# A decode attention backward kernel: scores by wide matmuls in four column groups, and another split of ten stores over the DMA engines

## The chip, the core and the metric

The kernel runs on one core of one Trainium2 chip. The metric is the device time of one execution in microseconds; the medians given are over ten runs. A core has a tensor engine (PE, with its weight loads shown apart as PEld), a vector engine (DVE), a scalar engine (ACT), GpSimd (POOL) and a sync engine (SP), and 16 DMA engines that move data between the HBM and the on-chip buffer. In this kernel SP issues the loads and POOL issues the stores. Matmul results land in a separate memory, PSUM[...].

## What is computed

The reference is the gradient of single-query attention. With 2 x 32 = 64 heads, one query row per head, 8192 keys and 128 elements per row, all in bfloat16, it returns the attention output and the gradients of q, k and v:

```python
def _fwd_reference(q, k, v):
    scale = q.shape[-1] ** -0.5
    scores = jnp.einsum("bhqd,bhkd->bhqk", q, k) * scale
    p = _softmax(scores, axis=-1)
    return jnp.einsum("bhqk,bhkd->bhqd", p, v)

def reference(q, k, v, grad_out):
    ...
    _out, _vjp = jax.vjp(_f, q, k, v)
    _grads = _vjp(grad_out)
```

Written out for one head: s = K q, E = exp(scale (s - max s)), l = sum E, p = E / l, dp = V g with g the row of grad_out, delta = sum(p dp), dS = p (dp - delta). The outputs are o = p V, dq = scale dS K, dk = scale dS q (an outer product, 8192 x 128) and dv = p g (likewise). K and V are read once, dk and dv written once: 268 MB each way.

## The kernel before

A head's K or V is one tile `kvt` of 128 partitions x 64 rows x 128 elements, 2 MB; partition p holds the keys 64 p to 64 p + 63. There are 12 such buffers (`NTILE`). A tile is loaded by one DMA of SP (`load`, L98), read by PE for the scores and for dq or o, then overwritten in place by DVE with the outer product dk or dv (`outer`, L394), and stored from there by one DMA of POOL (L412). The load of a later head waits for the store of the buffer that it takes. All instructions stand in program order on their engines (`pin`), and each engine runs its own queue in that order.

Time goes in slots: eight per head (`SL`), four for the K tile and four for the V tile, each on a chunk of 16 of the 64 row blocks. In a slot g the loop at L423 emits, in this order: loads that come due, one outer product of an earlier head, 16 PE transposes of the chunk into PSUM and one ACT copy to `ev` (`transpose_chunk`, L184 and L186), the partial sums for dq or o of an earlier head (`acc`, L339), the exponent (`expo`) when due, and the scores of the chunk of the slot before (`score_chunk`, L195). After these come the steps that are due once a head: maximum (`max_part`, `max_all`, `max_spread`), sums and weights (`normalise_p`, `weigh`, `normalise_ds`), and picking the dq or o sums out of PSUM (`pick`, then `join` two slots later).

The scores: each of the 16 transposed blocks in `ev` is loaded as weights and multiplied by the one column of q (or g) in `qdT`, 16 weight loads and 16 matmuls of one column a slot. The result for a chunk is 16 columns in the bank `sw` (scores) or `dpw` (dp), already in the layout in which the exponent wants them.

The sums for dq and o (`acc`): per slot four matmuls with 512 columns, whose weights are 64 columns of E or dS, taken from a zero-padded copy (`E_pad`, `dS_pad`); they go by turns to two groups of 64 output columns (`CW`, `NG`). `pick` takes the diagonal blocks out of the 512 columns with the 0/1 columns of `diag`, and `join` sums them over partitions.

Stores: eight of the 64 dk stores (`SPREAD`: heads 4, 11, ... 53) are issued in two parts by `by_rows` (L87), 126 partition rows and 2; all others are whole. The very first DMA of POOL resets the cursor from which its DMAs choose engines, and loads 6 rows of q (`FIRST`, L108 to L110). The last head's two tiles are stored in four pieces each by SP. At the end dq and o are transposed and each stored by one DMA of SP from 64 partitions (L489).

Of the kernel before, what the change touches and what calls it, by code (L numbers as in the profile page):

```python
# [13 lines left out]

CH = 16
QT = 4
CW = 64
NG = 2
NTILE = 12
FIRST = 6  # L20
SPREAD = range(4, 60, 7)

@with_exitstack
def kernel(
# [110 lines left out]
    nc.vector.memset(E_pad[:], 0.0)  # L136
    nc.vector.memset(dS_pad[:], 0.0)

    qdT = const.tile([P, 2, BH], BF16)
    for w in range(2):  # L140
        tps = ps_m.tile([P, BH], BF16, tag=f"acc{w}", name="tps")
        nc.tensor.transpose(tps[:], qd_nat[:BH, w, :], ident_bf[:BH, :BH])
        nc.vector.tensor_copy(out=qdT[:, w, :], in_=tps[:])

    dqT = const.tile([P, BH], BF16)
    oT = const.tile([P, BH], BF16)

    def begin_s(i):

        h = heads[i]  # L150
        sw = ps_sdp.tile([P, NT + P + 1], F32, tag="s", name="sw")
        h.s = sw[:, 0:NT]
        h.mT = sw[0:1, NT : NT + P]
        h.mb = sw[:, NT + P :]

    def begin_dp(i):

        h = heads[i]
        dpw = ps_sdp.tile([P, NT + 2 + D], F32, tag="dp", name="dpw")
        h.dp = dpw[:, 0:NT]  # L160
        h.lsum = dpw[:, NT : NT + 2]
        h.qbp = dpw[:, NT + 2 :]

    def broadcast(i, w):

        h = heads[i]
        pin(
            nc.tensor.matmul(  # L168
                h.qbp,
                lhsT=qdT[:, w, i : i + 1].to_broadcast([P, P]),  # L170
                rhs=ident_bf[:],
                start=True,
                stop=True,
            )
        )
        h.qb[w] = small.tile([P, D], BF16, tag=f"qb{w}", name="qb")
        pin(nc.vector.tensor_copy(out=h.qb[w][:], in_=h.qbp))  # L177
# [9 lines left out]
        return ev  # L187

    def score_chunk(i, c, ev):
        h = heads[i]  # L190
        w, c = divmod(c, NCH)
        dst = h.dp if w else h.s
        for t in range(CH):
            pin(
                nc.tensor.matmul(  # L195
                    dst[:, c * CH + t : c * CH + t + 1],
                    lhsT=ev[:, t, :],
                    rhs=qdT[:, w, i : i + 1],
                    start=True,
                    stop=True,  # L200
                )
            )
# [185 lines left out]
    def outer(i, w, c, ends):  # L388

        h = heads[i]  # L390
        n0 = c * CH
        shape = [P, CH, D // 2, 2]
        pin(
            nc.vector.tensor_tensor(  # L394
                out=h.tile[w][:, n0 : n0 + CH, :].rearrange("p n (e t) -> p n e t", t=2),
                in0=h.qb[w][:]
                .rearrange("p (e t) -> p e t", t=2)
                .unsqueeze(1)
                .to_broadcast(shape),
                in1=h.pair[w][:, n0 : n0 + CH, :].unsqueeze(2).to_broadcast(shape),  # L400
                op=ALU.mult,
            )
        )
        if c + 1 in ends:
            at = ends.index(c + 1)
            b0, b1 = (ends[at - 1] if at else 0) * CH, (c + 1) * CH
            dst = (dv_v if w else dk_v)[i]
            if w == 0 and i in SPREAD:
                by_rows(store_eng, dst, h.tile[w], (P - 2, 2))
            else:  # L410
                eng = load_eng if len(ends) > 1 else store_eng
                pin(eng.dma_start(out=dst[:, b0:b1, :], in_=h.tile[w][:, b0:b1, :]))  # L412
# [10 lines left out]
    for g in range(SL * BH + O0 + NCH + 4 - SL):  # L423
# [3 lines left out]
        def at(r0):  # L427

            return next((i for i, r in now if r == r0), None)
# [49 lines left out]
        if (i := at(A1 + NCH)) is not None:  # L479
            pick(i, 1)  # L480
# [39 lines left out]
```

## Time and profile before

| | us |
|---|---|
| median of 10 runs | 1286.93 |
| lowest, highest | 1285.25, 1289.36 |
| the profiled execution | 1284.91 |
| its span, first to last instruction | 1283.1 |

The profiled execution's time is 1.8 us over its span. The span is what views of the trace are timed in. The mean granted TensorE clock was 0.956.

| group | busy us | count, mean ns |
|---|---|---|
| L186 ACT copies of the transposed chunks | 954.4 | 512, 1865 |
| L394 DVE outer products | 621.9 | 512, 1215 |
| L184 PE transposes | 561.0 | 8192, 223 |
| L339 PE sums for dq and o | 168.6 + 159.9 | 2 x 1024, 412 and 393 |
| L195 PE scores | 141.9 + 140.7 | 2 x 4096, 164 |
| L362 DVE picking | 134.7 | 384, 351 |

The mean length of a PE record is longer than its share of busy time, because matmuls overlap in the pipeline. Queues of DMAs are named q0 (issued by POOL), q1 (issued by SP) and q8 (instructions); each is served by all 16 DMA engines at once, in packets of at most 16 KB, so that a whole load or store is 128 packets, eight for each engine. The page gives the mean busy share of the 16 engines in tenths for 40 slices of the span. A busy share by slice is a mean over the engines: it does not say whether one of them has more to do than another.

### The profile page before, as it was taken

The numbers are of one execution on the slowest core, as the hardware profiler recorded it, in microseconds if no ns is written. First come the engines' busy times: TensorE is split into PE (matmuls) and PEld (weight loads), VectorE is DVE, ScalarE is ACT, GpSimd is POOL, SyncE is SP. The second block draws the span as 40 slices with busy tenths as digits, with TensorE's granted clock in tenths as the row PEclk, the third lists the DMA queues.
The fourth block names the chain that finished last, engine by engine and source line by source line (L and its number), as shares of the span: only waits on it lengthen the run. The fifth ranks groups of instructions, "written<-read, shape, count | busy, mean of one in ns | idle before, by whom it ended". The sixth has DMA issues, their size and how long they took to land.

```text
span 1283.1 us, 42576 instructions
## 1 busy us (share of the span) xinstructions
PE 1131.4 (88%) x19268; PEld 860.5 (67%) x19268; DVE 936.0 (73%) x2122; ACT 975.2 (76%) x641; POOL 76.0 (6%) x143
## 2 busy tenths in 40 slices
PE   6999999999998989898888898897889899989881
PEld 5777777667766766676666676675667667767660
DVE  2888888778777867686777677776768677777773
ACT  6888888778777877786777787786778677777760
POOL 0000000000000000000000000000000000000000
PEclk9999999999999989998999999998999899999895
DMA  9999999999999999999999999999999999999996
GB/s 388 424 427 426 428 428 427 427 428 424 429 428 424 418 426 428 428 421 427 426 430 424 425 428 428 426 423 428 426 427 426 425 428 428 423 425 427 428 404 265
DMA packets 40194, 539.68 MB, mean 421 GB/s; under 512 B 5196, under 2 KB 5196, under 8 KB 6476
## 3 DMA queue, kind: packets, MB, share of 16 engines
q1 hardware_dynamic: 20172, 272.70, 49.9%
q0 software_dynamic: 19840, 264.25, 48.8%
q8 instruction: 150, 2.46, 0.7%
q14 instruction: 32, 0.26, 0.0%
HBM read 268.47 MB, written 268.47 MB: 418 GB/s over the span
## 4 chain that ended last, share of the span: by engine, by line
DMA 33%; another core or an unknown queue 30%; PE 19%; DVE 8%; issue 6%; ACT 2%; SPq 1%; POOL 0%; POOLq 0%; DVEq 0%; ACTq 0%
DMA kvt<-in_v_dram 20%; DMA kvt<-in_k_dram 9%; PE tp L184 8%; PE acc L339 5%; DVE kvt L394 5%; DMA out_dram<-kvt 3%; PE dpw L195 2%; PE sw L195 2%; ACT ev L186 1%; DVE sel L362 1%; SPq L98 1%; DMA qd_nat<-in_q_dram 1%; PE dpw L282 1%; DVE sel L356 0%
## 5 line engine op out<-in xcount | busy, mean ns | idle before, releaser
L186 ACT COPY ev<-tp 128x2048 bf16<-128x2048 bf16 x512 | 954.4, 1865 | 268.8 <-PE tp L184 257.2
L184 PE MATMUL tp<-ident_bf,kvt 128*128 128x128 bf16 x8192 | 561.0, 223 | 93.9 <-DMA kvt<-in_v_dram 77.8
L394 DVE TENSOR_TENSOR kvt<-qb,pair 128x2048 bf16<-128x2048 bf16 x512 | 621.9, 1215 | 0.3
L184 PEld LDWEIGHTS <-kvt 128*128 128x128 bf16 x8192 | 492.0, 101 | 100.6 <-DMA kvt<-in_v_dram 81.2
L195 PEld LDWEIGHTS <-ev 128*128 128x128 bf16 x8192 | 243.0, 96 | 209.3 <-issue 150.9
L339 PE MATMUL acc<-kvt,dS_pad 128*64 128x512 bf16 x1024 | 168.6, 412 | 1.6 <-DVE dqT L379 1.6
L339 PE MATMUL acc<-kvt,E_pad 128*64 128x512 bf16 x1024 | 159.9, 393 | 0.0
L195 PE MATMUL dpw<-qdT,ev 128*128 128x1 bf16 x4096 | 140.7, 164 | 17.9 <-DVE qb L177 17.1
L362 DVE SCALAR_TENSOR_TENSOR sel<-acc,diag,sel 128x128 f32<-128x128 f32 x384 | 134.7, 351 | 13.6
L195 PE MATMUL sw<-qdT,ev 128*128 128x1 bf16 x4096 | 141.9, 164 | 1.2 <-ACT ev L186 1.2
L207 DVE TENSOR_REDUCE mp<-sw 128x1 f32<-128x64 f32 x64 | 14.4, 225 | 161.6 <-PE sw L195 161.6
L412 POOL DMA_DIRECT2D out_dram<-kvt x118 | 63.3, 536 | 1082.5 <-DVE kvt L394 912.8
L339 PEld LDWEIGHTS <-dS_pad 128*64 128x64 bf16 x1024 | 37.7, 111 | 25.7 <-issue 6.3
L247 DVE CAST E_pad<-E_f 128x64 bf16<-128x64 f32 x64 | 12.5, 196 | 55.2 <-ACT E_f L238 55.2
L339 PEld LDWEIGHTS <-E_pad 128*64 128x64 bf16 x1024 | 36.2, 108 | 21.0 <-issue 0.2
L376 PE MATMUL acc<-ones,sel 128*128 128x1 f32 x256 | 43.3, 238 | 6.2 <-DVE sel L362 6.2
L282 PE MATMUL dpw<-ld,ones 128*128 128x1 f32 x256 | 46.3, 250 | 0.1
L356 DVE TENSOR_SCALAR sel<-acc,diag 128x128 f32<-128x128 f32 x128 | 44.1, 345 | 0.0
L376 PEld LDWEIGHTS acc<-ones,sel 128*128 128x128 f32 x256 | 39.0, 193 | 7.3 <-DVE sel L362 7.3
L253 DVE CUSTOM_DVE_ANT_0 junk<-E_f,dpw 128x64 bf16<-128x64 f32 x64 | 14.2, 221 | 39.1 <-PE dpw L195 39.1
L177 DVE CAST qb<-dpw 128x128 bf16<-128x128 f32 x128 | 35.6, 278 | 6.0 <-PE dpw L168 6.0
L282 PEld LDWEIGHTS dpw<-ld,ones 128*128 128x128 f32 x256 | 38.2, 189 | 0.5 <-DVE ld L253 0.5
(44 smaller groups left out, 314.8 us busy)
## 6 DMA issues: line engine op xcount, KB each, us to landing
out_dram<-kvt POOLq DMA_DIRECT2D x118, 2048.0 KB, 67.3
kvt<-in_v_dram SPq DMA_DIRECT2D x64, 2048.0 KB, 20.0
kvt<-in_k_dram SPq DMA_DIRECT2D x63, 2048.0 KB, 20.1
out_dram<-kvt POOLq DMA_DIRECT2D x8, 2016.0 KB, 72.5
out_dram<-kvt SPq DMA_DIRECT2D x8, 512.0 KB, 22.1
kvt<-in_k_dram SPq DMA_DIRECT2D x2, 512.0 KB, 4.5
kvt<-in_k_dram SPq DMA_DIRECT2D x1, 1024.0 KB, 7.1
out_dram<-kvt POOLq DMA_DIRECT2D x8, 32.0 KB, 71.9
```

What stands on the lines that cost most here:

```text
L177: pin(nc.vector.tensor_copy(out=h.qb[w][:], in_=h.qbp))
L184: pin(nc.tensor.transpose(tp[:, t, :], src[:, c * CH + t, :], ident_bf[:]))
L186: pin(nc.scalar.copy(out=ev[:], in_=tp[:]))
L195: nc.tensor.matmul(dst[:, c * CH + t : c * CH + t + 1], lhsT=ev[:, t, :], rhs=qdT[:, w, i : i + 1], start=True, stop=True,)
L207: pin(nc.vector.reduce_max(out=h.mp[:], in_=h.s, axis=AX.X))
L282: nc.tensor.matmul(out, lhsT=ones[:].to_broadcast([P, P]), rhs=col, start=True, stop=True)
L339: nc.tensor.matmul(h.acc[w][g : g + CW, :], lhsT=wts[:, n0 : n0 + CW], rhs=rows[:, n0 : n0 + QT, :].rearrange("p n d -> p (n d)"), start=( ...
L356: nc.vector.tensor_scalar(out=h.sel[:], in0=block, scalar1=diag[:, 0:1], scalar2=None, op0=ALU.mult)
L362: nc.vector.scalar_tensor_tensor(out=h.sel[:], in0=block, scalar=diag[:, b : b + 1], in1=h.sel[:], op0=ALU.mult, op1=ALU.add,)
L376: nc.tensor.matmul(h.acc[w][:, 0:1], lhsT=h.sel[:], rhs=ones[:], start=True, stop=True)
L394: nc.vector.tensor_tensor(out=h.tile[w][:, n0 : n0 + CH, :].rearrange("p n (e t) -> p n e t", t=2), in0=h.qb[w][:] .rearrange("p (e t) -> ...
L412: pin(eng.dma_start(out=dst[:, b0:b1, :], in_=h.tile[w][:, b0:b1, :]))
```

## The change

Four edits come together.

1. Scores. `score_chunk` no longer loads the transposed blocks as weights. The weights are 32 columns of a sparse `qdT`, in which the column of head i stands at place 3 + 4 i and zeros between, so that the window that begins at 3 + 4 i - c has the head's column at place c. For each of four groups g the 512 columns of `ev` blocks 4 g to 4 g + 3 are streamed through them into the 32 output rows of group g of a PSUM bank `raw`; the four chunks of a tile accumulate, each in its own row. After the fourth chunk `keep_raw` copies the bank (128 x 512 fp32) to SBUF by DVE, and in the next slot `spread_rows` brings it into the old layout by four fp32 matmuls against a one-hot `sel4`. Maximum, exponent, sums, `weigh` and `normalise_ds` each move one slot later; `begin` opens one bank for both score vectors in place of two.
2. Sums for dq and o: four groups of 32 output columns in place of two of 64.
3. Stores: ten dk stores (heads 4, 10, ... 58) in six DMAs each: 120 rows, 5 rows, and the last 3 rows in four quarters.
4. dq is stored in three DMAs (5, 44 and 15 rows), o in two (39 and 25).

```diff
-CW = 64
-NG = 2
+CW = 32
+NG = 4
+SG = 4
+SW = 32
 NTILE = 12
 FIRST = 6
-SPREAD = range(4, 60, 7)
+SPREAD = range(4, 60, 6)
...
+    sel4 = const.tile([P, NCH, SG], F32)
+    nc.vector.memset(sel4[:], 0.0)
+    for g in range(SG):
+        nc.vector.tensor_copy(
+            out=sel4[g * SW : (g + 1) * SW, :, g],
+            in_=ident_f[g * SW : (g + 1) * SW, g * SW : g * SW + NCH],
+        )
+
+    Q0 = NCH - 1
+    qdT = const.tile([P, 2, Q0 + NCH * BH + SW], BF16)
+    nc.vector.memset(qdT[:], 0.0)
...
+    def begin(i):
+
+        h = heads[i]
+        sw = ps_sdp.tile([P, 2 * NT + 2 * P + 4], F32, tag="s", name="sw")
+        h.score = (sw[:, 0:NT], sw[:, NT : 2 * NT])
+        h.s, h.dp = h.score
...
     def score_chunk(i, c, ev):
+
         h = heads[i]
         w, c = divmod(c, NCH)
-        dst = h.dp if w else h.s
-        for t in range(CH):
+        if c == 0:
+            h.raw = ps_sdp.tile([P, QT * P], F32, tag="raw", name="raw")
+        q0 = Q0 + NCH * i - c
+        for g in range(SG):
             pin(
                 nc.tensor.matmul(
-                    dst[:, c * CH + t : c * CH + t + 1],
-                    lhsT=ev[:, t, :],
-                    rhs=qdT[:, w, i : i + 1],
+                    h.raw[g * SW : (g + 1) * SW, :],
+                    lhsT=qdT[:, w, q0 : q0 + SW],
+                    rhs=ev[:, g * QT : (g + 1) * QT, :].rearrange("p n d -> p (n d)"),
+                    start=(c == 0),
+                    stop=(c == NCH - 1),
+                )
+            )
+
+    def keep_raw(i):
+
+        h = heads[i]
+        h.rows = work.tile([P, QT * P], F32, tag="rows", name="rows")
+        pin(nc.vector.tensor_copy(out=h.rows[:], in_=h.raw[:]))
+
+    def spread_rows(i, w):
+
+        h = heads[i]
+        for t in range(QT):
+            pin(
+                nc.tensor.matmul(
+                    h.score[w].rearrange("p (n t) -> p n t", t=QT)[:, :, t],
+                    lhsT=h.rows[:, t * P : (t + 1) * P],
+                    rhs=sel4[:].rearrange("p c g -> p (c g)"),
                     start=True,
                     stop=True,
                 )
...
             if w == 0 and i in SPREAD:
-                by_rows(store_eng, dst, h.tile[w], (P - 2, 2))
+                by_rows(store_eng, dst, h.tile[w], (P - 8, 5))
+                for b in range(NCH):
+                    r = (slice(P - 3, P), slice(b * CH, (b + 1) * CH))
+                    pin(
+                        store_eng.dma_start(
+                            out=dst[r], in_=h.tile[w][r], max_dma_last_dim=CH * D
+                        )
+                    )
...
-            if r == 0:
-                begin_s(i)
-            if r == 3:
-                begin_dp(i)
+            if r == NCH:
+                begin(i)
                 broadcast(i, 1)
-            if r == 6:
+            if r == NCH + 2:
                 broadcast(i, 0)
...
-        if (i := at(NCH + 2)) is not None:
+        if (i := at(NCH + 1)) is not None:
+            spread_rows(i, 0)
+        if (i := at(SL + 1)) is not None:
+            spread_rows(i, 1)
+        if (i := at(NCH + 3)) is not None:
             max_spread(i)
             expo(i)
...
         if (i := at(NCH)) is not None:
+            keep_raw(i)
+        if (i := at(SL)) is not None:
+            keep_raw(i)
+        if (i := at(NCH + 1)) is not None:
             max_part(i)
-        if (i := at(NCH + 1)) is not None:
+        if (i := at(NCH + 2)) is not None:
             max_all(i)
-        if (i := at(NCH + 3)) is not None:
+        if (i := at(NCH + 4)) is not None:
             normalise_p(i)
-        if (i := at(SL)) is not None:
+        if (i := at(SL + 1)) is not None:
             weigh(i)
-        if (i := at(SL + 1)) is not None:
+        if (i := at(SL + 2)) is not None:
             normalise_ds(i)
...
-        load_eng.dma_start(out=dst.rearrange("b h s d -> (b h s) d"), in_=nat[:BH, 0, :])
+        rows = dst.rearrange("b h s d -> (b h s) d")
+        p = 0
+        for m in (5, 44, 15) if w == 0 else (39, 25):
+            load_eng.dma_start(out=rows[p : p + m], in_=nat[p : p + m, 0, :], max_dma_last_dim=D)
+            p += m
```

More of the change, by code (lines that the diff above doesn't have):

```diff
@@ L137 @@
     nc.vector.memset(dS_pad[:], 0.0)
-    qdT = const.tile([P, 2, BH], BF16)
+    sel4 = const.tile([P, NCH, SG], F32)
[8 more added lines that the diff above has]
+    nc.vector.memset(qdT[:], 0.0)
     for w in range(2):
@@ L142 @@
         nc.tensor.transpose(tps[:], qd_nat[:BH, w, :], ident_bf[:BH, :BH])
-        nc.vector.tensor_copy(out=qdT[:, w, :], in_=tps[:])
+        nc.vector.tensor_copy(
+            out=qdT[:, w, Q0 : Q0 + NCH * BH].rearrange("p (i f) -> p i f", f=NCH)[:, :, 0],
+            in_=tps[:],
+        )
     dqT = const.tile([P, BH], BF16)
     oT = const.tile([P, BH], BF16)
-    def begin_s(i):
+    def begin(i):
         h = heads[i]
[L151 to L162, printed above, removed]
+        sw = ps_sdp.tile([P, 2 * NT + 2 * P + 4], F32, tag="s", name="sw")
+        h.score = (sw[:, 0:NT], sw[:, NT : 2 * NT])
+        h.s, h.dp = h.score
+        h.mT = sw[0:1, 2 * NT : 2 * NT + P]
+        h.qbp = sw[:, 2 * NT + P : 2 * NT + 2 * P]
+        h.lsum = sw[:, 2 * NT + 2 * P : 2 * NT + 2 * P + 2]
+        h.mb = sw[:, 2 * NT + 2 * P + 2 : 2 * NT + 2 * P + 3]
     def broadcast(i, w):
@@ L169, in broadcast @@
                 h.qbp,
-                lhsT=qdT[:, w, i : i + 1].to_broadcast([P, P]),
+                lhsT=qdT[:, w, Q0 + NCH * i : Q0 + NCH * i + 1].to_broadcast([P, P]),
                 rhs=ident_bf[:],
@@ L408, in outer @@
             if w == 0 and i in SPREAD:
-                by_rows(store_eng, dst, h.tile[w], (P - 2, 2))
+                by_rows(store_eng, dst, h.tile[w], (P - 8, 5))
[5 more added lines that the diff above has]
+                        )
+                    )
             else:
```

## The prediction

> **What bounds the kernel now.** I read the page first, then the waits of SP's queue, then windows over the end of the span, and last the single DMA packets of the trace. From the page:
>
> ```profile
> span 1283.1 us, 42576 instructions
> PE 1131.4 (88%) x19268; PEld 860.5 (67%) x19268; DVE 936.0 (73%) x2122; ACT 975.2 (76%) x641; POOL 76.0 (6%) x143
> ...
> DMA  9999999999999999999999999999999999999996
> ...
> q1 hardware_dynamic: 20172, 272.70, 49.9%
> q0 software_dynamic: 19840, 264.25, 48.8%
> q8 instruction: 150, 2.46, 0.7%
> ...
> out_dram<-kvt POOLq DMA_DIRECT2D x118, 2048.0 KB, 67.3
> kvt<-in_v_dram SPq DMA_DIRECT2D x64, 2048.0 KB, 20.0
> ```
>
> The 16 DMA engines are busy in every slice. Loads (q1) and stores (q0) share them half and half; q8, instructions, is small. A store lands 67.3 us after its issue, so about seven stores are always queued: a store issued a few us later costs nothing. SP's queue says the same:
>
> ```profile
> SPq L98 <- DMA out_dram<-kvt: 1138.9, 116, 24.2
> ```
>
> SP waits almost the whole span for a stored buffer to come free. Compute is faster: where nothing holds it, every eighth copy of L186 (one head) starts 17.31 us after the last, while the mean over 62 heads is (1224.8 - 25.9)/62 = 19.3 us. The windows show where DMA time is lost:
>
> ```profile
> 420.00:1200.00 780.00, 694.33 (x11768) 528.15 (x11766) 571.25 (x1290) 595.09 (x392) 45.92 (x83) 0.96 1.01 426
> ...
> 1240.00:1252.00 12.00, 9.12 (x113) 5.50 (x110) 10.37 (x25) 4.26 (x5) 0.53 (x1) 0.85 0.86 365
> 1252.00:1263.00 11.00, 4.22 (x18) 1.79 (x14) 8.76 (x17) 0.00 (x0) 0.00 (x0) 0.50 0.98 404
> 1263.00:1274.00 11.00, 0.00 (x0) 0.00 (x0) 0.00 (x0) 0.00 (x0) 0.00 (x0) 0.50 0.55 228
> 1274.00:1282.00 8.00, 0.00 (x0) 0.00 (x0) 0.00 (x0) 0.00 (x0) 0.00 (x0) 0.50 0.36 146
> ```
>
> The last column but one is the DMA share. Compute ends at 1263, and then for 18 us about half of the engines, and at the end 7 of 16, still move data. Some engines have more to do than others, and the last of them ends the run.
>
> Which ones? A packet of 16 KB takes 611 ns, and the next one on its engine starts 4 ns before it ends, so the packets can be strung into 16 chains by their times (labels can swap where two engines end together, so I use classes of engines). My own tally, with rows of 16 KB worked out from the stores' shapes:
>
> ```
> class                      engines  rows  q8 packets  mean row   last busy, us of the span
> with fetches                  7     2056     18-19     615 ns    1280-1281, no gap before
> without fetches               7     2056       0       613 ns    1263-1267, dry about 1241-1247
> relieved, with fetches        1     1992      18       620 ns    by 1273
> relieved, without fetches     1     1992       0       636 ns    by 1273
> ```
>
> Every q8 packet falls on one of eight engines, in turn. It costs its engine 1.37 us (mean of 148: from its start to that of the fifth packet after it, less 607 ns for each row between), because the row beside it is slowed too. So a fetching engine needs 2056 x 0.607 + 18.8 x 1.37 = 1248 + 25.8 = 1274 us, plus 2 for semaphore packets and 4 for a slow start from 1.8: it ends at 1281, as measured. These seven are the bound. One engine is slow by itself (839 of its rows take over 635 ns); the eight split stores take 7 rows each from it and from its neighbour.
>
> **What the skill says.** "DMA: Bandwidth & Descriptors", Why a DMA increments its semaphore by 16 and not by 1: a DMA uses the largest k up to 16 that divides its outer dimension, and on POOL's path k below 16 means k consecutive engines from a cursor. The trace agrees: 14 chains have 144 packets of 8 KB (8 stores x 9 rows x 2) and two have 16. "Runtime: NRT & Kernel Launch", Instruction fetch mechanics: a sequencer fetches blocks of 16 KiB, 256 instructions, over its own DMA queue. It agrees: 2 x 19268 PE records / 256 = 150.5, and q8 has 150 packets. "TensorEngine Tiling (Array Packing)", Tiling Modes: with outputs of 32 columns there are four tiles that run in parallel. The trace has two groups only: at 602 us two L339 matmuls start 3 ns apart and the next pair 240 ns later.
>
> **The change part by part.**
>
> Instruction stream. L195 loses 16,384 PE instructions; the new scores bring 2 x 2048 = 4096; the one-hot matmuls are 512 in fp32, each two weight loads and two matmuls by the records of L282 (256 of each for 128 calls): 2048. So 38,536 - 16,384 + 4096 + 2048 = 28,300, 110.5 blocks, 13.8 for each fetching engine in place of 18.8: 5.0 x 1.37 = -6.9 us each.
>
> Stores. Of the old split store 126 rows went on 14 engines (9 each) and 2 on the other two. Now k is 15 for 120 rows (8 each), 5 for 5, and 3 for each quarter of the last 3 rows. The q load of 6 rows leaves the cursor at 6 (the relieved pair are among the six engines that carry that load in the trace); 120 rows leave out engine 5, the five rows go to 5-9, the quarters to 10-12, 13-15, 0-2, 3-5, and the cursor is at 6 again. Per store: engine 5 has 1.25 rows, 6-9 have 9, the others 8.25. Over ten stores, against 2048 even rows: -67.5, +10, +2.5. Before, it was -56 for engines 4 and 5 and +8 for the others.
> - Fetching engine in 6-9 (two, if fetchers alternate as 3 of the first 6 suggest): +2 rows, +1.2 us. Fillers and semaphores, six DMAs for two, some 110 packets of 6 ns: +0.7. With the fetches: -5.0 us.
> - Other fetching engines: -5.5 rows = -3.3, fetches -6.9, small packets +0.5: -9.7 us.
> - The slow engine, if it is 5: -11.5 rows x 0.634 = -7.3 us from a place that was not last. Not the bound.
> - Engine 4, if a fetcher, gets 58.5 rows back, +35.5 - 6.9, and is then like the other fetchers.
>
> POOL's queue. Stores share eight semaphores, and each waits for the one eight issues earlier (the trace: 110.3 us in 14 waits of L412 on out_dram). A split store now takes six, so its last piece waits for the store three before it and the next store for the one two before: by 67.3 us to landing and 9.7 us between stores, POOL stands up to 67 - 19 = 48 us, with the following stores behind it. Queue 0 then still holds two stores, 19 us of work, so I price it at 0. Lower bound 0; if the two ran out, up to a few us at each of ten places.
>
> PE. Out: L195, 141.9 + 140.7 us busy. In: scores 512 x 0.24 us (four groups together; 0.48 if only pairs). L339 loses one of two 240 ns steps: -123 us (0 if only pairs). One-hot: 512 x 0.22 us (L282's passes start 110 ns apart) = 113; at its recorded 250 ns for each of two passes, 256. Net -170; at worst +220. DVE: 128 copies of 128x512 from PSUM: L177 takes 278 ns for 128 columns, L316 to L362 adds 67 ns for 64: 278 + 384 x 1.05 = 0.68 us, 87 us in all (96 if counted up from L362's 351 ns). DVE becomes 1023 us, 16.0 a head. Exponent, sums and p come one step later; L339 starts where it did. I take 17 to 18.5 us a head, hidden under 19.3. If that cover goes, each us a head costs 63.
>
> The end. Five small output DMAs for two: under 0.3 us, on queues with 15 us of backlog.
>
> Sum: what ends last are the two fetching engines in 6-9, -5.0 us. The profiled execution, 1284.91 us (span 1283.1), would be 1279.9; the median shown is 1286.93, so the forecast is 1281.9.
>
> **Rivals.**
> - B, slower: the slow engine is not 5 but 4. The trace gives no engine numbers, only that it is one of the relieved pair. It would then carry 2050.5 rows x 0.634 = 1300 us, plus 5 for the start (1992 x 0.634 = 1263 ends at 1268 or later now): 1305, 24 past the present end, so 1311 us. It decides from (1281 - 5) / 0.634 = 2013 rows, that is if it keeps fewer than 35 of its 56 rows of relief. For it: nothing tells the pair apart by place. Against: the other of the pair is only a fetcher, in no need of more relief than its seven fellows.
> - C, slower: compute becomes the bound. For: DVE at 16.0 of 17.3 us, new PE-DVE-PE steps in one in-order queue. Against: PE gets lighter, two us of slack. At 19.7 us a head compute ends 62 x 0.4 = 25 us later, at 1288, and with some 8 us of transfers behind it the time is about 1300; it decides from 19.5.
> - D, no change: POOL's waits let queue 0 run dry on the fetching engines, or the row slowed beside a fetch was slow for another reason, and 3 to 5 us are eaten: 1286.
> - The relief not doing what it says (k other than 15) would leave 120 rows even on 16 engines and the slow one unrelieved: part of B.
>
> **How the numbers follow.** 0.2% is 2.6 us, about what a measurement here can tell. Forecast 0.71 (own range 1277, where all fetchers count as "other", to 1284), D 0.11, B 0.10, C 0.08. Faster 0.71, same 0.11, slower 0.18. The range 1277 to 1289 holds the first two and leaves out B and C.
>
> **What would show it.** q8 near 110 packets; compute done by about 1263 as before; the DMA share falling to about 2 of 16 engines for the last 4 us, those ending at 1276 of the span, the other fetching engines at 1271; heads at 17-18.5 us where undisturbed. Wrong, if one engine alone runs for 20 us and more at the end (B), if L186 waits for PE or DVE over 2 us a head more (C), or if the mid-span DMA share falls under 1.00 (D).

## The result, and the profile after

The changed kernel takes 1314.28 us (median of 9 runs, 1310.77 to 1320.31) where the kernel before, run beside it, takes 1286.79 us (31 runs). The ratio is 1.0215, with a 95% interval of 1.0204 to 1.0226: slower by 27.5 us. The forecast was 1281.9 us. The profiled execution took 1310.77 us, the lowest of the nine. From its page:

```profile
span 1309.0 us, 32556 instructions
...
PE 1104.3 (84%) x14148; PEld 807.8 (62%) x14148; DVE 1015.5 (78%) x2258; ACT 958.1 (73%) x641; POOL 99.7 (8%) x185
...
GB/s 389 428 429 427 429 427 428 427 419 428 429 419 398 429 427 405 383 430 426 368 425 429 418 371 428 430 422 390 429 425 414 398 430 423 371 427 428 420 374 277
...
q0 software_dynamic: 21216, 264.26, 48.4%
q8 instruction: 110, 1.80, 0.5%
...
out_dram<-kvt POOLq DMA_DIRECT2D x116, 2048.0 KB, 36.6
```

The instruction fetches fell from 150 to 110 as forecast, and PE and DVE have slack. But the line of GB/s has dips that recur every third or fourth slice from slice 13 on, about 120 us apart: that is the distance of the split stores. A store now lands 36.6 us after its issue, not 67.3: fewer stores stand in the queue. A long stretch in the middle and then the end, by windows (columns: length, busy time of PE, PEld, DVE, ACT and POOL, then granted clock, DMA share, GB/s):

```profile
420.00:1200.00 780.00, 669.66 (x8624) 489.98 (x8621) 618.83 (x1369) 584.78 (x391) 60.82 (x109) 0.95 0.99 413
...
1240.00:1263.00 23.00, 20.25 (x280) 15.19 (x279) 19.94 (x44) 17.91 (x12) 3.22 (x6) 1.00 0.86 356
1263.00:1276.00 13.00, 8.04 (x53) 4.27 (x52) 11.10 (x27) 2.29 (x4) 0.53 (x1) 0.60 0.99 415
1276.00:1290.00 14.00, 2.78 (x14) 1.40 (x14) 6.85 (x13) 0.00 (x0) 0.00 (x0) 0.50 1.01 424
1290.00:1300.00 10.00, 0.00 (x0) 0.00 (x0) 0.00 (x0) 0.00 (x0) 0.00 (x0) 0.50 0.77 307
1300.00:1308.00 8.00, 0.00 (x0) 0.00 (x0) 0.00 (x0) 0.00 (x0) 0.00 (x0) 0.50 0.06 21
```

A DMA share of 0.06 is one engine of sixteen: one alone ends the run. By a count of the packets under way it is alone with rows of data for some 7 us, from 1298.5 to 1305.8. Followed back from its last packet for 40 to 50 us, it carried no fetch, and about half of its rows of 16 KB took over 620 ns. That is how the slow engine looks. The other engines are late too: the share is still 0.77 between 1290 and 1300.

The waits of POOL's queue for earlier stores changed as well (in total, times, longest), first before and then after:

```profile
POOL out_dram L412 <- DMA out_dram<-kvt: 110.3, 14, 14.5
```

```profile
POOL out_dram L446 <- DMA out_dram<-kvt: 223.8, 28, 9.6
...
POOL out_dram L452 <- DMA out_dram<-kvt: 47.1, 4, 14.0
```

L446 issues the quarters of a split store. It alone waits 223.8 us for earlier stores, where all of POOL's waits on stores before were 110.3.

To see which engine each split store spares, I strung the packets into 16 chains again, afresh around each split store. A row is two packets of 8 KB in these stores; "slow rows" are rows over 635 ns in the 60 to 90 us around it. The whole table is a tally of my own.

```
kernel                     8-KB packets of the engine   spared engine: 8-KB      first packet of the slow
                           with 29-49 slow rows         packets, its slow rows   engine after the earliest
after                      16 in nine of ten stores,    2, 0-9                   3 and 8 us, then 18-21 us
                           the tenth unclear
after, FIRST = 5 (e1)      2 in ten of ten              the same engine          11-14 us
```

So the relief misses its engine: the slow one carries its full eight rows of each split store, and an engine with ordinary rows is spared. From the third split store on the slow engine reaches each some 20 us after the first engine.

### The profile page after: what moved, and what is told of

It reads as the page before. It is cut to its first block, busy times and chain, and to the rows that moved or that the text cites. A ratio compares the mean times of both kernels' runs of the same rounds, so it can differ in the third digit from the quotient of the medians.

```text
span 1309.0 us, 32556 instructions
## 1 busy us (share of the span) xinstructions
PE 1104.3 (84%) x14148; PEld 807.8 (62%) x14148; DVE 1015.5 (78%) x2258; ACT 958.1 (73%) x641; POOL 99.7 (8%) x185
## 4 chain that ended last, share of the span: by engine, by line
DVE 39%; DMA 21%; PE 15%; ACT 11%; another core or an unknown queue 8%; issue 3%; POOL 0%; SPq 0%; ACTq 0%; DVEq 0%
DVE kvt L427 22%; DMA kvt<-in_v_dram 15%; ACT ev L196 10%; PE tp L194 9%; DVE sel L395 5%; DMA out_dram<-kvt 5%; DVE rows L221 4%; PE acc L372 2%; DVE sel L389 2%; DVE pair L303 1%; PE raw L208 1%; ACT E_f L271 1%; DVE dSu L349 1%; PE sw L178 1%
## 5 line engine op out<-in xcount | busy, mean ns | idle before, releaser
L194 PE MATMUL tp<-ident_bf,kvt 128*128 128x128 bf16 x8192 | 575.5, 226 | 62.8 <-DMA kvt<-in_v_dram 51.3
L194 PEld LDWEIGHTS <-kvt 128*128 128x128 bf16 x8192 | 509.0, 103 | 184.8 <-issue 111.2
L208 PE MATMUL raw<-ev,qdT 128*32 128x512 bf16 x2048 | 210.8, 401 | 4.4 <-ACT ev L196 1.6
L228 PEld LDWEIGHTS sw<-sel,rows 128*128 128x128 f32 x1024 | 126.0, 194 | 29.8 <-issue 13.9
L228 PE MATMUL sw<-sel,rows 128*128 128x16 f32 x1024 | 138.4, 267 | 0.0
L372 PE MATMUL acc<-kvt,E_pad 128*32 128x512 bf16 x1024 | 103.3, 393 | 28.6 <-DVE E_pad L280 28.5
L221 DVE COPY rows<-raw 128x512 f32<-128x512 f32 x128 | 87.7, 685 | 50.9 <-PE raw L208 50.9
L372 PE MATMUL acc<-kvt,dS_pad 128*32 128x512 bf16 x1024 | 111.8, 428 | 0.8 <-DVE dS_pad L358 0.8
L178 PE MATMUL sw<-ident_bf,qdT 128*128 128x128 bf16 x128 | 28.6, 224 | 66.0 <-DVE mp L240 66.0
L208 PEld LDWEIGHTS <-qdT 128*32 128x32 bf16 x2048 | 64.1, 95 | 22.8 <-issue 16.5
L315 PEld LDWEIGHTS sw<-ld,ones 128*128 128x128 f32 x256 | 38.4, 189 | 54.9 <-issue 29.7
L372 PEld LDWEIGHTS <-E_pad 128*32 128x32 bf16 x1024 | 26.4, 93 | 53.1 <-DVE E_pad L280 37.6
L315 PE MATMUL sw<-ld,ones 128*128 128x1 f32 x256 | 49.3, 262 | 0.1
## 6 DMA issues: line engine op xcount, KB each, us to landing
out_dram<-kvt POOLq DMA_DIRECT2D x116, 2048.0 KB, 36.6
```

What stands on the lines that cost most here:

```text
L194: pin(nc.tensor.transpose(tp[:, t, :], src[:, c * CH + t, :], ident_bf[:]))
L208: nc.tensor.matmul(h.raw[g * SW : (g + 1) * SW, :], lhsT=qdT[:, w, q0 : q0 + SW], rhs=ev[:, g * QT : (g + 1) * QT, :].rearrange("p n d -> ...
L221: pin(nc.vector.tensor_copy(out=h.rows[:], in_=h.raw[:]))
L228: nc.tensor.matmul(h.score[w].rearrange("p (n t) -> p n t", t=QT)[:, :, t], lhsT=h.rows[:, t * P : (t + 1) * P], rhs=sel4[:].rearrange("p ...
L315: nc.tensor.matmul(out, lhsT=ones[:].to_broadcast([P, P]), rhs=col, start=True, stop=True)
L372: nc.tensor.matmul(h.acc[w][g : g + CW, :], lhsT=wts[:, n0 : n0 + CW], rhs=rows[:, n0 : n0 + QT, :].rearrange("p n d -> p (n d)"), start=( ...
```

## The experiments

The runs are named e1 to e17. All 17 kernels compute everything. They ran in six groups, each on another chip of the same kind; the kernel before, run in each group, gave medians of 1286.2 to 1287.6 us. Readings of single packets are tallies of my own from the profiled execution of each kernel.

**The slow engine's place.** If the slow engine is 4, counted from 0 at the cursor's reset, the cursor must start one earlier:

```diff
-FIRST = 6
+FIRST = 5
```

> The changed kernel with FIRST = 5: the cursor starts at 5, so 120 rows leave out engine 4, and every other share shifts down by one. Theory B (the slow engine is 4 and lost its relief): it gets back 67.5 rows x 0.63 us, no longer ends last, and the time falls to about 1282 to 1290, whatever the compute rate allows; no single engine is busy alone for the last 8 us. Theory C (compute at 19 us a head is the bound): 1308 to 1316 as in the changed kernel, with the last transposes at the same time. Theory D (POOL's eight store semaphores let queue 0 run dry): 1308 to 1316 too, with the dips of the DMA share at the split stores unchanged.

Measured: 1285.70 us (20 runs, 1283.97 to 1296.55), ratio 0.9996 (0.9983 to 1.0009). One digit gives back 28.6 us. It ends 4 us above the forecast of 1281.9. Its profiled execution is the slowest of the twenty, 1296.55 us, so readings of that trace stand for a worse case than the median.

The counterpart spoils the relief of the kernel before, whose hole is two engines wide, 4 and 5 with `FIRST` at 6:

```diff
-FIRST = 6
+FIRST = 7
```

> The kernel before with FIRST = 7 and nothing else: the two relieved engines become 5 and 6, and engine 4 gets 8 rows more than even. Theory B: engine 4 carries 2056 rows x 0.634 = 1303 us plus 5: +27 us, 1311 to 1317. If the slow engine is 5, or none is slow for itself, within 3 us of before. Theories C and D: no difference, 1285 to 1289, since compute and the number of DMAs are the same.

Measured: 1314.55 us (1312.78 to 1316.67), ratio 1.0219 (1.0200 to 1.0237). The two together place the slow engine at 4.

**Halves of the change.** First the kernel before with the ten new stores alone, then the new scores and sums with the eight old stores:

```diff
-                by_rows(store_eng, dst, h.tile[w], (P - 2, 2))
+                by_rows(store_eng, dst, h.tile[w], (P - 8, 5))
+                for b in range(NCH):
...
```

> The kernel before with the new split of ten stores alone (120, 5, 4 x 3 quarter rows, FIRST = 6). Theory B: the slow engine carries 2050.5 rows in place of 1992, +58.5 x 0.634 = 37 us on that engine, +24 on the end: 1309 to 1313. Theory C: compute is untouched, so within 3 us of before, 1287 or a little more. Theory D: the stores land 67 us after issue here, two stores stay queued, so 1287 to 1292.

Measured: 1326.20 us, ratio 1.0312 (1.0291 to 1.0333): 13 us above the upper end. The slow engine alone does not make that much.

> The changed kernel with the old eight split stores (126 and 2 rows), so the new scores and sums with the old relief of engines 4 and 5. Theory B: only the fetches fall, 40 blocks fewer over eight engines, 5 x 1.37 = -6.9 us: 1279 to 1284. Theory C: heads at 19 us set the pace and the time stays at 1300 to 1315. Theory D: two DMAs a split store as before, so no more stall than before: 1279 to 1290.

Measured: 1281.04 us (1280.06 to 1286.05), ratio 0.9964 (0.9948 to 0.9980). The same kernel again:

> The same kernel as the one with new scores and sums and the old stores, in more rounds, to have an interval that tells it from the kernel before and from the three-DMA stores beside it: 1279 to 1284, ratio 0.994 to 0.998.

Measured: 1283.37 us (1279.49 to 1287.18), ratio 0.9974 (0.9962 to 0.9986). With the old stores this half brings what was forecast of it. From the first of its two profiles, POOL's wait on stores, and then the windows over the end:

```profile
POOL out_dram L445 <- DMA out_dram<-kvt: 24.6, 2, 13.5
```

```profile
1255.00:1265.00 10.00, 0.90 (x3) 0.63 (x3) 2.87 (x8) 0.00 (x0) 0.00 (x0) 0.50 0.77 321
1265.00:1275.00 10.00, 0.00 (x0) 0.00 (x0) 0.00 (x0) 0.00 (x0) 0.00 (x0) 0.50 0.42 169
1275.00:1279.00 4.00, 0.00 (x0) 0.00 (x0) 0.00 (x0) 0.00 (x0) 0.00 (x0) 0.50 0.04 16
```

No engine stays behind alone for long, and POOL hardly waits for stores.

**Which edit brings the gain.** Sums alone (`CW = 32`, `NG = 4` in the kernel before), and scores alone (`CW = 64`, `NG = 2`, old stores):

> The kernel before with the sums for dq and o in four groups of 32 columns and nothing else changed. Theory 1 (the bound is the DMA engines that carry the fetches, and the number of instructions does not change): 1285 to 1289, 150 fetches, while undisturbed heads fall from 17.3 us to 15 to 16.5. Theory 2 (compute does bound a part of the span, so a lighter PE brings time): under 1284.

Measured: 1286.64 us, ratio 1.0003 (0.9993 to 1.0013): nothing. The lines of its two groups of L339, which before took 168.6 and 159.9 us:

```profile
L339 PE MATMUL acc<-kvt,E_pad 128*32 128x512 bf16 x1024 | 116.3, 445 | 0.0
L339 PE MATMUL acc<-kvt,dS_pad 128*32 128x512 bf16 x1024 | 113.5, 435 | 2.0 <-DVE dqT L379 2.0
```

These two groups fall by 99 us, and the time does not move. But PE as a whole did not get lighter. Its busy time, and that of the transposes, which took 561.0 us before:

```profile
PE 1130.4 (88%) x19268; PEld 930.1 (73%) x19268; DVE 940.2 (73%) x2124; ACT 965.5 (75%) x641; POOL 76.0 (6%) x143
...
L184 PE MATMUL tp<-ident_bf,kvt 128*128 128x128 bf16 x8192 | 646.5, 243 | 78.8 <-DMA kvt<-in_v_dram 70.2 <-DMA kvt<-in_k_dram 8.4
```

The sum before was 1131.4 us. The granted clock is 0.816 to 0.852 in all twelve runs, where the kernel before has 0.946 to 0.967 beside them, and the transposes are longer by 85 us. So the unchanged time of this run does not by itself show that PE was not the bound. Its undisturbed heads do: they take some 16.0 us (17.31 before), under the 19.3 us of the mean.

> The kernel before with the new scores alone: sums in two groups of 64 columns and the eight old split stores stay. Theory 1 (the gain of new scores and sums together is the 40 fetches saved, and compute has slack either way): 1279 to 1284, 110 fetches. Theory 2 (the head of 19.1 us with both edits already stands just under the 19.3 us that the transfers allow, so that the sums' faster PE is what keeps compute hidden): PE gets some 113 us back, 1.7 us a head if PE is what sets the head, undisturbed heads 20 us and more, and the time is 1300 to 1370.

> The same kernel as the one with the new scores alone (sums in two groups, old split stores), in more rounds: 1279 to 1284, ratio 0.993 to 0.998. It tells whether the new scores alone do all that scores and sums together do (1281.0 and 1283.4).

Measured: 1279.43 us, ratio 0.9954 (0.9936 to 0.9971), and again 1280.29 us (12 runs, 1277.79 to 1287.68), ratio 0.9952 (0.9939 to 0.9965). The whole gain is that of the scores, and this kernel beats both that the study began with. But in it compute has caught up. From its page, and the transposes:

```profile
PE 1190.1 (93%) x14148; PEld 810.8 (63%) x14148; DVE 1025.7 (80%) x2256; ACT 975.3 (76%) x641; POOL 76.0 (6%) x143
...
q8 instruction: 110, 1.80, 0.5%
...
PE 67%; DVE 18%; ACT 11%; issue 3%; DMA 1%; ACTq 0%; SPq 0%; DVEq 0%
...
L194 PE MATMUL tp<-ident_bf,kvt 128*128 128x128 bf16 x8192 | 544.6, 220 | 0.0
```

In its chain of waits 67% of the span is PE. Each head after the first takes 19.4 to 19.6 us, nearly all of them 19.44, and the last figure of L194 says that PE never waits for a load (93.6 us of such waits before). So in this kernel compute sets the pace through the whole middle of the run, at almost the 19.3 us that the transfers took a head before.

**No split store at all**, in the kernel before and in the kernel after:

```diff
-SPREAD = range(4, 60, 6)
+SPREAD = ()
```

> The kernel before with no split store: every engine carries 2048 rows, and every store is one DMA. If the slow engine is bound by its rows at 0.634 to 0.640 us each: 2048 rows are 1298 to 1311 us, plus 5 to 7, less the 2 that a slow start does not cost twice: 1304 to 1316. It lies under the kernel before with FIRST at 7 (about 2056 rows on that engine, 1314.6) by 8 rows, some 5 us: 1309 is what I expect. If the split stores themselves, and not the rows on the slow engine, made that kernel slow: under 1295.

Measured: 1303.99 us (1303.55 to 1306.22). Relief is worth 17 us to the kernel before; the eight rows that part it from the kernel with `FIRST` at 7 cost 10.6 us, twice their 5.

> The kernel after with no split store at all: new scores, new sums, every store one DMA, 2048 rows on every engine, 110 fetches. Theory 1 (the slow engine, which carries no fetch, is the bound without relief, and the changed kernel's 1314 is this and the cost of six DMAs a store): as the kernel before without split stores, 1304, so 1301 to 1307, which leaves some 10 us of the 1314 to the six DMAs, of which 2.5 rows of 0.634 are 1.6. Theory 2 (the six DMAs cost the changed kernel nothing, its slow engine is busy all the while): 1314 less 1.6, so 1310 to 1315.

Measured: 1294.99 us (1294.48 to 1295.68), ratio 1.0061 (1.0042 to 1.0080). The time is below both theories. The changed kernel is 19.3 us faster without its relief. The end:

```profile
1240.00:1263.00 23.00, 19.75 (x252) 14.37 (x244) 17.33 (x38) 16.98 (x12) 1.06 (x2) 0.93 0.56 236
1263.00:1276.00 13.00, 6.72 (x50) 3.61 (x49) 11.10 (x28) 1.75 (x3) 0.53 (x1) 0.67 0.68 282
1276.00:1290.00 14.00, 2.51 (x14) 1.12 (x14) 6.22 (x12) 0.00 (x0) 0.00 (x0) 0.50 0.54 212
1290.00:1293.00 3.00, 0.00 (x0) 0.00 (x0) 0.00 (x0) 0.00 (x0) 0.00 (x0) 0.50 0.02 7
```

From 1240 us on nearly half of the engines are idle: the others are ahead with their work, and the slow one is behind. In the changed kernel the share there was 0.86 to 1.01: all were late.

**Half of the split stores** (`SPREAD = range(4, 60, 12)`, five in place of ten):

> The kernel after with five of its ten split stores (at heads 4, 16, 28, 40, 52). With ten it takes 1314.3, with none 1295.0; the slow engine's rows are 2049 here. In the traces the slow engine never stands still, but has 36 rows over 800 ns with ten split stores and 4 with none. Theory 1 (each split store of six DMAs costs the slow engine some 1.8 us, as the engines ahead of it run dry and start again beside it): about half way, 1302 to 1308, and about 20 such rows. Theory 2 (the loss comes from the slow engine's lag reaching a limit, whatever the number of splits): near 1312.

Measured: 1300.36 us (1297.91 to 1303.32), ratio 1.0108 (1.0092 to 1.0124), a little under the first theory's range. It rules out the second theory, a limit that is reached whatever the number. Nor is it an equal price for each store: five cost 5.4 us, and ten, which lie half as far apart, cost 19.3. The lines of GB/s, first with five split stores, then with none:

```profile
GB/s 389 427 427 427 428 429 427 429 428 429 428 413 413 427 430 427 430 427 424 358 415 427 429 427 428 429 395 364 429 430 427 429 428 425 353 425 427 429 427 248
```

```profile
GB/s 390 423 429 429 427 429 427 429 428 429 428 428 428 428 428 428 430 428 429 428 429 429 427 428 429 429 428 429 428 417 426 429 420 426 427 405 428 408 290 207
```

Four of the five stores have their dip; without them the line stays level until slice 29.

What does such a store do to the slow engine? In windows of 80 us from 40 to 1240 us of each trace I took the chain with most rows of 635 to 800 ns, and its rows. Chains can swap within a window, so the figures are approximate:

```
kernel                              mean row   rows over   their excess over    gaps
                                    all, ns    800 ns      the others, us       us
before, no split store (e11)         636.5        4             1.2             0.0
new scores and sums, old stores (e3) 631.6        2             0.8             0.0
after, no split store (e15)          631.7        4             1.3             0.0
after, five split stores (e16)       634.0       19             9.0             7.1
after                                640.0       36            17.9             1.9
before, ten new stores (e2)          645.8       59            21.8             4.6
```

The slow engine hardly stands still, but ten split stores give it 32 more rows over 800 ns, together 16.6 us. In the trace of the changed kernel such rows come in bunches on many engines at once: at 530.6 to 531.1 us of the span eight rows of 1208 ns, where rates had just dipped. Adding up: 1295.0 for the slow engine with 2048 rows, 2.5 more rows at 0.632 us are 1.6, and 16.6 of stretched rows make 1313.2; measured 1314.3. The two profiled executions, at 1310.8 and 1295.7, lie only 15.1 us apart, so the sum is good to some 3 us.

**The number of DMAs in a split store.** The next runs were to tell whether POOL's eight semaphores make that loss. The first has three DMAs and the hole at 4:

```diff
-                by_rows(store_eng, dst, h.tile[w], (P - 8, 5))
-                for b in range(NCH):
...
+                pin(store_eng.inc_swdge_sem([], [], mode="reset_dge_cursor"))
+                by_rows(store_eng, dst, h.tile[w], (5, P - 8, 3))
```

> The kernel after, with each of its ten split stores as three DMAs in place of six: a reset of POOL's engine cursor, then 5 rows (engines 0 to 4), 120 rows (5 to 15 and 0 to 3), 3 rows (4 to 6). Engine 4 has 2 rows of such a store, in place of 8.25: 60 rows less over ten stores, against 56 in the kernel before. Theory 1 (the slow engine is 4; and what the kernel with FIRST at 5 still loses against the old stores comes from POOL waiting, because six DMAs of one store use up its eight semaphores): 1278 to 1283, mid-span idle time of the DMA engines (20 to 1240 us) near 1 us as with the old stores, POOL's wait of the split store for an earlier store well under the 193 us of the kernel with FIRST at 5. Theory 2 (the five us come from the relief itself, rows that go to others, or from the ten stores in place of eight, not from semaphores): 1284 to 1288 and idle time of several us. If the slow engine is not 4: 1305 and above.

Measured: 1299.25 us (6 runs, 1288.07 to 1307.91), ratio 1.0079 (1.0048 to 1.0110). Neither theory. Its idle time from 20 to 1240 us is 0.9 us, as the first wanted, and the slow engine carries 4 packets of 8 KB in place of 16 or 18. But the end is another engine's:

```profile
1265.00:1275.00 10.00, 0.90 (x3) 0.63 (x3) 1.27 (x5) 0.00 (x0) 0.00 (x0) 0.50 0.58 236
1275.00:1285.00 10.00, 0.00 (x0) 0.00 (x0) 0.00 (x0) 0.00 (x0) 0.00 (x0) 0.50 0.16 63
1285.00:1294.00 9.00, 0.00 (x0) 0.00 (x0) 0.00 (x0) 0.00 (x0) 0.00 (x0) 0.50 0.06 23
```

Followed by its chain, an engine with fetches and nine rows of each split store falls back: 12 us behind the first at 372 us of the span, 31 at 598, 52 at 942. Its 8-KB packets between 372 and 840 us took 407 ns on average by my tally, where those of the old stores take 309 to 332. Why is open.

With the hole left at 5 (`(6, P - 8, 2)` after the reset):

> The kernel after with the hole left at engine 5, but each split store as three DMAs: a reset of the cursor, then 6 rows (engines 0 to 5), 120 rows (all but 5), 2 rows (5 and 6). Engine 4 has 9 rows of each, 2058 in all, 7.5 more than in the changed kernel; nothing in it uses up POOL's semaphores. It tells how the changed kernel's loss divides. Theory 1 (both parts add up: the slow engine's rows at the price of the kernel with no split store, 1304 for 2048 rows, and the rest of the changed kernel's 1314.3 from six DMAs a store): 1304 + 10 x 0.634 = 1310, so 1307 to 1313, with idle time well under the changed kernel's 17 us. Theory 2 (the slow engine's rows alone made the 1314.3, and the idle time of the others cost nothing): 1314.3 + 7.5 x 0.634 = 1319, so 1317 to 1322. The loss that hit the three-DMA kernel with the hole at 4 ended at 1299 on another engine and is hidden here.

Measured: 1313.79 us (4 runs, 1309.79 to 1321.51). The runs cover both theories. The profiled one, at the lower end, gives the slow engine 19 rows over 800 ns with 7.3 us of excess, fewer than with six DMAs.

Then the old stores cut by columns, into six and into four DMAs:

```diff
-                by_rows(store_eng, dst, h.tile[w], (P - 2, 2))
+                for n0, n1 in ((0, NT // 2), (NT // 2, 3 * NT // 4), (3 * NT // 4, NT)):
+                    for r in (slice(0, P - 2), slice(P - 2, P)):
+                        pin(
+                            store_eng.dma_start(
+                                out=dst[r, n0:n1],
+                                in_=h.tile[w][r, n0:n1],
+                                max_dma_last_dim=NT * D,
...
```

> New scores and sums with the eight old split stores (126 rows and 2 rows), each of the two DMAs cut into three by columns: one half and two quarters. The engine cursor moves 14 and 2 for each cut, 48 in all, so the same engines carry the same rows as with the old stores and the relief is theirs; only the number of DMAs, six in place of two, is that of the changed kernel. Theory 1 (six DMAs of one store use up POOL's eight semaphores, so that the engines can stand only some 34 us apart where they reach a split store, in place of 60, and the ones ahead run dry): POOL waits more for earlier stores, the first to the last packet of a split store lie within about 35 us, DMA idle time from 20 to 1240 us is 3 us or more, and the time is 1283 to 1290. Theory 2 (the count of DMAs costs nothing, and the changed kernel's dips are the work of its unrelieved slow engine alone): 1279 to 1283, idle time near 1 us.

> New scores and sums with the eight old split stores, each of the two DMAs cut into two halves by columns: four DMAs a store, with the same engines carrying the same rows. With two DMAs it took 1281 to 1283.4, with six 1299.2. Theory 1 (the cost is that of POOL's eight semaphores: the more of them one store takes, the less far apart the engines can stand): between the two, 1284 to 1296, the last of the splits some 45 to 55 us from its first packet to its last. Theory 2 (the cost with six is that of smaller packets, the quarters): halves have packets of 8 KB as the old stores do, 1280 to 1284.

Measured: 1299.24 us (1297.86 to 1302.31) with six, 1299.85 (1299.40 to 1313.88) with four. Both expectations rest on a wrong premise: the chains show that a cut of 126 rows puts eight on each of fifteen engines and six on the last. The slow engine has its eight rows, the relief is gone, and the runs are to be read beside the 1295.0 with no split store. So eight cut stores add 4 to 5 us, and six DMAs no more than four.

> New scores and sums with eight split stores of three DMAs that start with a reset of the cursor: 6 rows (engines 0 to 5), 112 rows (6 to 15 and 0 to 3), 10 rows (4 to 13). Engines 4 and 5 have 2 rows, as they have none to 7 fewer in the old stores: nearly the old relief. The three-DMA stores with a reset and a hole at 4 alone took 1299 where 1281 was expected. Theory 1 (the reset or the third DMA costs that time by itself): 1292 to 1303 here too. Theory 2 (it was the hole at one engine, with the rest of the rows uneven): 1280 to 1286.

Measured: 1304.35 us (1300.34 to 1305.86). The premise fails here too: 112 is 16 times 7, so these rows went to all engines, and the chains show 16 packets on each. It is another kernel without relief, 9 us over the one with no split store.

So these runs, read beside the kernels with no split store, tell what split stores of different forms cost an unrelieved slow engine. The loss is the time over the kernel with no split store and the same scores, less 0.632 us (old scores: 0.637) for each row over 2048. The third column is the time from the first to the last 8-KB packet of one split store, from the fifth store on. The fourth is the mean idle time of the 16 engines between 20 and 1240 us.

```
split stores x DMAs               loss us,   8-KB packets    idle
                                  a store    spread over us  us
after, 10 x 6                     1.8        31-35           17
five of them, 5 x 6 (e16)         0.9        37              12
old scores, 10 x 6 (e2)           2.1        30-36           23
cut by columns, 8 x 6 (e9)        0.5        31-37            6
cut by columns, 8 x 4 (e13)       0.6        59-61            2
with a reset, 10 x 3 (e12)        1.2        61-67            3
with a reset, 8 x 3 (e14)         1.2        59-66            1
old scores, 8 x 2 (e4)            0.7        69-72            6
```

The third column shows what six DMAs do: engines that could lie 59 to 72 us apart with two to four DMAs are held to 30 to 37, as the expectation for e9 said. The engines idle more as well. But the loss does not go with either: e9 has the narrow spread and loses 0.5 us a store, e14 has a wide spread, hardly any idle time, and loses 1.2.

Last, ten of the old split stores in place of eight, with the new scores and sums:

> New scores and sums with ten of the old split stores (126 rows and 2 rows) in place of eight. It tells whether it is the number of split stores that cost the kernel with FIRST at 5 and the one with three DMAs their time. If the count is harmless: the slow engine has 14 rows less, the fourteen others 2 more, 1280 to 1284. If each split store costs by itself (slow rows around it): 1285 and above.

Measured: 1283.39 us (14 runs, 1279.77 to 1294.30), about the same as with eight (1281.04 and 1283.37). The number of split stores is harmless while each is two DMAs with the relief in the right place.

## Why the prediction was wrong

- The step that failed is "The slow engine, if it is 5: ... Not the bound". The trace left two candidates, a pair of neighbours, and the sum took one of them. With nothing to tell the pair apart, rival B's chance of 0.10 was too small. It is 4. The changed kernel spares 5, which needed nothing, so the slow engine becomes the bound. The two runs that move `FIRST` show it in both directions (28.6 us back, 28 us lost), and the chains of nine split stores show the engine itself.
- Rival B had this mechanism and a fitting time, 1311, but its sum was wrong inside. It priced 2050.5 rows at 0.634 us; in the new kernel they are 0.632, and 2048 of them end at 1295.0, not at 1309. The rest of the 1314.3, some 18 us, is the split stores' doing. That its time came so near is luck. Its sign, one engine alone for 20 us and more, did not come: it was some 7. Rival D's sign did, a mid-span DMA share under 1.00: it was 0.99 between 420 and 1200 us.
- That is the second wrong term: the POOL step, "I price it at 0". The bound from above, a few us at each of ten places, held: some 1.8 us each. The reasoning that covered it, that queue 0 "still holds two stores, 19 us of work", took the engines for level. In the traces they drift apart: the 8-KB packets of one old split store spread over 17 us at the first and 61 us at the last. An engine 20 us ahead has used up two stores. With the new stores the slow engine reaches each split store 18 to 21 us after the first engine from the third on, which is those two stores at 9.7 us. My reading was that dry engines start again beside the slow one, whose rows then stretch. The waits of L446, the dips and the stretched rows of this kernel fit that. It is not shown, and it can't be all: split stores of three DMAs (e12, e14) cost 1.2 us each with engines that idle 1 to 3 us in all. Shown is that six DMAs a store hold the engines closer together and let them run dry, that the split stores cost the time, by the run without them, and that five cost less than ten. How a split store slows the slow engine stays open.
- With the hole at 4 much of the waits remains (193.2 us at L446, in the slowest execution) and the time is 1285.7, against 1281.0 to 1283.4 with the old stores. Rival D's 1286, at its chance of 0.11, describes that kernel.
- Fetches: -6.9 us for each fetching engine. Measured on the scores alone, 6.8 and 6.2 us; no run changes the number of fetches by itself, so that they are the cause is argued, not shown. "Runtime: NRT & Kernel Launch", Instruction fetch mechanics, held for the count: 28,296 PE records are 110.5 blocks of 256, and q8 has 110 packets.
- DVE: 0.68 us a copy and 1023 us in all. Measured 685 ns and 1015.5 us. Four column groups run together: at 601.75 us four matmuls of L372 start 3 to 4 ns apart, and L372 takes 103.3 + 111.8 us, where two groups took 328.5. The new scores were sized at 123 us and take 210.8, and PE as a whole fell by 27 us (1131.4 to 1104.3), not by 170. These lines of the changed kernel's groups carry that (busy time, mean of one, idle before):

```profile
L208 PE MATMUL raw<-ev,qdT 128*32 128x512 bf16 x2048 | 210.8, 401 | 4.4 <-ACT ev L196 1.6
...
L372 PE MATMUL acc<-kvt,E_pad 128*32 128x512 bf16 x1024 | 103.3, 393 | 28.6 <-DVE E_pad L280 28.5
L221 DVE COPY rows<-raw 128x512 f32<-128x512 f32 x128 | 87.7, 685 | 50.9 <-PE raw L208 50.9
```

- Rival C, compute as the bound, did not come true, but "17 to 18.5 us a head" was too low: with new scores and sums and the old stores heads 12 to 36 take 19.1 us, and a store lands after 49.9 us in place of 67.3. The cover is nearly gone, and with the new scores alone it is gone: 19.44 us a head is just under the 19.5 from which C decides. The sums in four groups bring no time today; with them PE is busy 86% of the span (e3) and not 93% (e7), although the granted clock is lower, 0.94 in place of 0.99.

## What to carry to other kernels

Where a relief is aimed at one of several like units by a counter, find out which one it is before narrowing the aim: undo or shift the counter by one and measure. A queue that sixteen engines share must cover their drift, not their mean: a queue of "two stores" is empty for the engine that is two stores ahead. When one part of the work on an engine gets cheaper, look at the granted clock and at the engine's whole busy time before calling the engine lighter. And where a form of DMA is changed, by a cut in columns or another count of rows, count its packets for each engine before reading the time.

## What the runs showed of the hardware

- How a DMA's rows go to the engines depends on its form. Whole rows in DMAs of 126 or 120 went to 14 or 15 engines, as "DMA: Bandwidth & Descriptors", Why a DMA increments its semaphore by 16 and not by 1, gives it for POOL's path; the same 126 rows cut by columns went to 16 engines, eight each and six on the last. The page has an exception of this kind for some copies, with the rows divided by 16 and rounded up, and the trace agrees.
- The slow engine's rows took 636.5 ns on average with the old scores and 631.7 with the new, although it carries no fetch in either (e11 and e15, no split store): 9.0 us of time. The two ran on different chips, but a difference between the old and the new scores shows on one chip too: rows of 680 to 720 ns between 40 and 1240 us, on all engines, are 159 with the old scores (e6) and 40 with the new (e7). Nothing here shows why.
- The granted clock goes with the form of the matmuls. On one chip the kernel before has 0.946 to 0.967, the sums in four groups alone 0.816 to 0.852 (e6), the new scores alone 0.989 to 0.992 (e7), both together 0.932 to 0.944 (e8).
- The kernels with three DMAs a split store spread most from run to run: 1288 to 1308 us in six runs with the hole at 4, 1310 to 1322 in four with the hole at 5, against 1294.5 to 1295.7 in four with no split store.
